# Attention in three units of 128-token chunks in place of four of 96, beside a PE-bound pair of feed-forward layers

## The chip, the core and the metric

The kernel runs on one core of one Trainium2 chip. The metric is the device time of one execution in microseconds. TensorE is called PE here, VectorE DVE, ScalarE ACT; SyncE (SP) issues the transfers.

## What is computed

Attention with pooled keys and values (each 8 tokens are averaged, so 576 tokens leave 72 keys), for 8 batches of 8 heads with a head size of 64, and then two feed-forward layers over all 4608 tokens, one with a leaky ReLU, one with a hard swish. All inputs are fp32, and the feed-forward products are made as three products of rounded parts (high x high, high x low, low x high).

```python
k_p = k.reshape(B, H, Sp, pool, D).mean(axis=3)
v_p = v.reshape(B, H, Sp, pool, D).mean(axis=3)
scores = scale * np.matmul(q, k_p.transpose(0, 1, 3, 2))
scores = scores - np.max(scores, axis=-1, keepdims=True)
attn = np.exp(scores)
attn = attn / (np.sum(attn, axis=-1, keepdims=True) + 1e-09)
attn_out = np.matmul(attn, v_p)
x = np.ascontiguousarray(attn_out.transpose(0, 2, 1, 3)).reshape(B * S, H * D)
h = x @ w_in;   x = np.maximum(0.01 * h, h) @ w_out
h = x @ w2_in;  y = (h * np.clip(h + 3.0, 0.0, 6.0) / 6.0) @ w2_out
```

## The kernel before

**Units.** `Unit(b, g, h)` is the attention of batch b, four heads (group g) and half of the tokens (h, 288 of 576). There are four to a batch, 32 in all. A unit has three chunks of `CQ` = 96 tokens. `scores` makes 12 small fp32 matmuls (3 chunks, 2 pairs of heads, 2 heads of a pair in the two halves of PE's rows), 96 queries as weights against 72 pooled keys, into two PSUM banks with the tag `a`. DVE takes the maxima (L484) and multiplies them by -1/64 (L489), ACT makes 12 exponentials with the sum of each row (L495, two instructions each: `ACTIVATE` and a read of the accumulator) into an SBUF tile `sm`, and DVE inverts the sums and scales the exponentials. `transposes` turns 64 of the 72 key columns (2 x 3 transposes, L545), `transpose_rem` the other 8 (3, L563), and `values` multiplies with the values (2 x 4 matmuls 288 wide, L590; in the first batch 2 x 2, one of them in full fp32).

**Preparation.** The first unit of a batch in each group (`fresh`) brings keys and values and pools them: `prep_k` reduces the keys into the group's one tile `keys`, and `prep_v` the values into `vbd` and `vrm`. The first batch pools its values on PE (`pool_v`, L400).

**Feed-forward layers.** A token tile of 512 tokens goes through 16 weight blocks f: `gemm1` (12 matmuls, L712 to L714) and `gemm2` (12, L761 to L763). The first two tiles start before their attention is whole: some blocks (`half0`, `half1` of them) are run first on the columns 0 to `HALF` and later on the rest, `HALF` to 512. The later tiles run in pairs with seven products in place of eight (`left_right`, L1016).

**Order.** The program is written as a list of tasks; `Plan.order` places them on the engines with assumed costs, so the order of each engine follows from the costs and from the slots in `C` at which attention steps are put between weight blocks (`att0` to `att7`, with the gaps of a unit's five steps). PE works strictly in its order. Up to the first `gemm2` the plan fills PE's expected idle time with matmuls on a tile of zeros (`plan.fill`, L1565), one for each 56 ns.

Of the kernel before, what the change touches and what calls it, by code (L numbers as in the profile page):

```python
# [21 lines left out]
POOL, SP = 8, 72  # L22
NF = DFF // 128
HALF, CQ, NC = 288, 96, 3
# [6 lines left out]
    n32=4,  # L31
    soon={0: 8000, 1: 4000},
    flex=562,
# [3 lines left out]
    when0=[0, 1, 0, 4, 9, 12, 17],  # L37
    att0=[0, 0, 13, 37],
    sec0=4,
    half1=4,  # L40
    steps1='frrffrfffffffrff',
    when1=[3, 15, 16, 20],
    att1=[0, 0, 27, 30],
    sec1=6,
    att2=[2, 4],
    quick=[0, 2, 2, 2, 2],
    slow=[0, 3, 3, 5, 3],
    left1=[[(0, 0), (1, 8)], [(2, 0), (3, 6)]],
    att3=[0, 0, 6, 9, 12, 13, 18, 21],
    gaps3=[0, 3, 3, 3, 0],  # L50
    prep3=[28, 37],
    att5=[5, 15, 24, 33, 42, 51, 60, 69],
    gaps5=[0, 7, 5, 11, 5],
    prep5=[77, 100],
    att7=[9, 24, 37, 55],
    gaps7=[2, 10, 10, 10, 12],
    prep7=[80, 85],
    left2=[[(0, 10)], [(1, 17)], [(2, 32)], [(3, 26), (4, 44), (5, 60)], [(6, 5), (7, 37)]],
)
SCORES = 1200  # L60
# [190 lines left out]
def attention_moe_moe(ctx: ExitStack, tc: tile.TileContext, qt, kt, vm, vr, wt, wq, eye, mask, out):  # L251
# [82 lines left out]
    class Unit:  # L334


        def __init__(self, b, g, h):
            self.b, self.g, self.h = b, g, h
            self.fresh = h == 0
            self.early = b == 0 and h == 0  # L340
            self.tag = "sb" if (g and b < 5) else "s"
            self.whole32 = None

# [17 lines left out]
    def fetch(u):  # L361
        if u.early:
            for i in range(2):
                load(half_k(u, i), kt[u.b, u.g, :, 576 * i : 576 * i + 576], 294912)
        elif u.fresh:
            load(u.k, kt[u.b, u.g], 589824)
        load(u.q, qt[u.b, u.g, u.h], 294912)
        if u.fresh:
            load(u.v, vm[u.b, u.g], 524288)
            load(u.r, vr[u.b, u.g], 196608)  # L370
# [21 lines left out]
    def pool_v(u):  # L392

        ps = buf("h", [128, 512], F32, 2, psum)
        u.vs, u.rs = ps("v", lambda t: t[:, 0:128]), ps("r", lambda t: t[:CQ, 128:192])
        for src, dst, n in ((u.v, u.vs, 128), (u.r, u.rs, 64)):

            def emit(src=src, dst=dst, n=n):
                for i in range(POOL):
                    PE.matmul(  # L400
                        out=dst.ap(),
                        lhsT=ident.ap()[: dst.ap().shape[0], : dst.ap().shape[0]],
                        rhs=src.ap()[:, i * n : i * n + n],
                        start=i == 0,
                        stop=i == POOL - 1,
                    )

            on_pe(1740 if n == 128 else 1320, emit, [src, ident], [dst])

    held_keys, held_values = {}, {}  # L410

    def prep_k(u):
        held_keys[u.g] = u.b
        k = View(keys[u.g].buf, None, lambda t: t.rearrange("p a n -> p (a n)"))
        if u.early:
            for i in range(2):
                sum_pool(part(keys[u.g], i, lambda t, i=i: t[:, i, :]), half_k(u, i), 72)
        else:
            sum_pool(k, u.k, 144)

    def prep_v(u):
# [7 lines left out]
        for e in range(2):  # L429
            p = slice(64 * e, 64 * e + 64)  # L430
            s = View(u.vs.buf, u.vs.key, lambda t, p=p: pair(u.vs.cut(t))[p])
            if u.whole32:
                copy(part(u.whole32[0], e, lambda t, p=p: t[p, :, p]), s, 128, u.early)
                continue
# [19 lines left out]
    def scores(u):  # L454


        assert held_keys[u.g] == u.b
# [3 lines left out]
        sm = buf("sm", [CQ, 12], F32, 2)  # L461
        at = lambda: s.get()[:CQ, 0 : NC * 4 * SP].rearrange("p (c h k) -> p c h k", c=NC, h=4)
        pss = [buf("a", [128, 512], F32, 2, psum) for _ in range(2)]

        def emit():
            for c in range(NC):
                for pi in range(2):
                    for e, ps in enumerate(pss):
                        rows = slice(64 * e, 64 * e + 64)
                        PE.matmul(  # L470
                            out=ps.get()[:CQ, (2 * c + pi) * SP : (2 * c + pi) * SP + SP],
                            lhsT=u.q.ap()[rows, pi * HALF + c * CQ : pi * HALF + c * CQ + CQ],
                            rhs=keys[u.g].ap()[rows, pi, :],
# [4 lines left out]
        on_pe(SCORES, emit, [u.q, keys[u.g]], [ps() for ps in pss])  # L478
        for e, ps in enumerate(pss):
            s4 = lambda ps=ps: ps.get()[:CQ, 0:432].rearrange("p (c a k) -> p c a k", c=NC, a=2)  # L480
            m = mx(e, lambda t, e=e: t[:, :, e : e + 3 : 2])
            on_dve(
                432,
                lambda m=m, s4=s4: DVE.tensor_reduce(out=m.ap(), in_=s4(), op=ALU.max, axis=AX.X),  # L484
                [ps()],
                [m],
            )

            on_dve(6, lambda m=m: DVE.tensor_scalar_mul(m.ap(), m.ap(), -1.0 / 64.0), [m], [m])  # L489

            def exps(e=e, s4=s4):
                for c in range(NC):
                    for pi in range(2):
# [5 lines left out]
                            scale=1.0 / 64.0,  # L499
# [4 lines left out]
            add("act", 1782, exps, [ps(), m], [s(e), sm(e)])  # L504
        whole = [s(pi) for pi in range(2)]
        inv = buf("inv", [CQ, 12], F32, 2)()
        on_dve(12, lambda: DVE.tensor_scalar_add(inv.ap(), sm.get(), 1e-9), [sm()], [inv])
# [16 lines left out]
        flat = lambda: s.get()[:CQ, 0 : NC * 256]  # L524
# [10 lines left out]

    def transposes(u):
        u.t = []
        pss = []
        for pi in range(2):
# [3 lines left out]
            def emit(ps=ps, pi=pi):  # L543
                for c in range(NC):
                    PE.transpose(out=ps.get()[:, c * CQ : c * CQ + CQ], in_=u.p(c, pi), identity=ident.ap()[:CQ, :CQ])  # L545

            on_pe(281, emit, [*u.whole, ident], [ps()])
        for pi, ps in enumerate(pss):
            src = ps(None, lambda t: t[:, 0:HALF])
            if u.whole32:  # L550
                copy(u.whole32[1][pi], src, HALF, True)
# [6 lines left out]
    def transpose_rem(u):  # L558
        ps = buf("a", [128, 512], F32, 2, psum)

        def emit():
            for c in range(NC):
                PE.transpose(  # L563
                    out=ps.get()[:96, c * CQ : c * CQ + CQ],
                    in_=f32(u.rem.get()[:, c].rearrange("p a b -> p (a b)")),
                    identity=ident.ap()[:CQ, :CQ],
                )

        on_pe(277, emit, [u.rem(), ident], [ps()])
# [3 lines left out]
    def values(u, x, spill):  # L573
        assert held_values[u.g] == u.b
        vh, vl = [t() for t in vbd[u.g]]
        pss = []
        for pi in range(2):
            ps = buf("a", [128, 512], F32, 2, psum)
            pss.append(ps)
            if u.whole32:  # L580
                ops = [(u.whole32[0], u.whole32[1][pi])]
            else:
                th, tl = u.t[pi]
                ops = [(vh, th), (vh, tl), (vl, th)]
            ops = [(l, lambda l=l, pi=pi: l.ap()[:, pi, :], r) for l, r in ops]
            ops.append((vrm[u.g](), lambda pi=pi: vrm[u.g].get()[:, 128 * pi : 128 * pi + 128], u.tr))

            def emit(ps=ps, ops=ops):
                for i, (_, l, r) in enumerate(ops):
                    PE.matmul(out=ps.get()[:, 0:HALF], lhsT=l(), rhs=r.ap(), start=i == 0, stop=i == len(ops) - 1)  # L590

            on_pe(536 if len(ops) > 2 else 609, emit, [v for l, _, r in ops for v in (l, r)], [ps()])
        for pi, ps in enumerate(pss):
            k = 2 * u.g + pi

            if u.h == 0:
                dst = x((k, 0), lambda t, k=k: t[:, k, 0:HALF])
                copy(dst, ps(None, lambda t: t[:, 0:HALF]), HALF, True, 0.125)
            else:
                n = TOK - HALF  # L600
                dst = x((k, 1), lambda t, k=k: t[:, k, HALF:TOK])
                copy(dst, ps(None, lambda t, n=n: t[:, 0:n]), n, True, 0.125)
                dst = spill(k, lambda t, k=k: t[:, k, :])
                copy(dst, ps(None, lambda t, n=n: t[:, n:HALF]), REST, True, 0.125)
# [727 lines left out]
    def attend(jobs, u, slot, held, nxt, gaps):  # L1332
# [4 lines left out]
        def first():  # L1337
            scores(u)
# [4 lines left out]
        at(s[0], first)  # L1343
        at(s[1], lambda: transposes(u))
        at(s[2], lambda: transpose_rem(u))
        at(s[3], lambda: values(u, held["x"], held["spill"]))
        if nxt is not None:
            at(s[4], lambda: prepare(nxt))
# [6 lines left out]
    units = [Unit(b, g, h) for b in range(B) for h in range(2) for g in range(2)]  # L1355
# [4 lines left out]
    u0, u1, u2, u3 = units[:4]  # L1360
    place(u0)
    u1.q = a15("q", lambda t: t[:, 1296:1872])
    raw_k(u1, a15)
    raw_v(u1, a14)
    for u in units[: C["n32"]]:
        g = u.g
        a = a13 if g else a12
        v = a("v", lambda t: pair(t[:, 0:256]))
        u.whole32 = v, [a(("p", i), lambda t, i=i: t[:, 256 + 288 * i : 544 + 288 * i]) for i in range(2)]
        if u.early:  # L1370
            add("gp", 400, lambda v=v: GP.memset(v.ap(), 0.0), [], [v])
    u2.q, u3.q = a7("q2", lambda t: t[:, 0:576]), a7("q3", lambda t: t[:, 576:1152])
# [41 lines left out]
    fetch(u3)  # L1414
# [21 lines left out]
    attend_all(jobs, (2, 3), C["att0"][:2], held, QUICK)  # L1436
# [17 lines left out]
    attend_all(jobs, (4, 5), C["att0"][2:], held, SLOW)  # L1454
# [9 lines left out]
    attend_all(jobs, (6, 7), C["att1"][:2], held, QUICK)  # L1464
# [3 lines left out]
    attend_all(jobs, (8, 9), C["att1"][2:], held, SLOW)  # L1468
# [9 lines left out]
    attend_all(jobs, (10, 11), C["att2"], held, SLOW)  # L1478
# [11 lines left out]
    def attend_batch(jobs, b, slots, gaps, store, begin=None, chain=False):  # L1490

        held = {}
        units_of = units[4 * b : 4 * b + 4]
# [18 lines left out]
        for n, (u, slot) in enumerate(zip(units_of, slots), 1):  # L1512
            nxt = units_of[n] if n < 4 else units[4 * b + 4] if chain else None
# [23 lines left out]
    attend_batch(jobs, 3, C["att3"][:4], C["gaps3"], True, chain=True)  # L1537
    held = attend_batch(jobs, 4, C["att3"][4:], C["gaps3"], False)
# [7 lines left out]
    attend_batch(jobs, 5, C["att5"][:4], C["gaps5"], True, 0, True)  # L1546
    held = attend_batch(jobs, 6, C["att5"][4:], C["gaps5"], False)
# [76 lines left out]
```

## Time and profile before

| | |
|---|---|
| runs | 1585.05, 1589.53, 1590.87 us |
| median | 1589.53 us |
| span of the profiled execution | 1583.1 us |
| its own time | the page doesn't give it; the runs lie 2.0 to 7.8 us above the span |
| PE busy | 1572.4 us (99%), 8312 matmul passes |
| DVE busy | 1184.9 us (75%) |
| ACT busy | 999.7 us (63%) |
| granted clock of PE | 1.000 of 2.4 GHz over the span |

A matmul's recorded length holds its way through the array, so lengths of neighbours overlap and "busy" can hide small waits. What an instruction costs PE in a row of its like is the distance between two starts. Attention is spread over the first 653 us; the rest of the span is feed-forward work alone.

### The profile page before, as it was taken

The numbers are of one execution on the slowest core, as the hardware profiler recorded it, in microseconds if no ns is written. First come the engines' busy times: TensorE is split into PE (matmuls) and PEld (weight loads), VectorE is DVE, ScalarE is ACT, GpSimd is POOL, SyncE is SP. The second block draws the span as 40 slices with busy tenths as digits, with TensorE's granted clock in tenths as the row PEclk, the third lists the DMA queues.
The fourth block names the chain that finished last, engine by engine and source line by source line (L and its number), as shares of the span: only waits on it lengthen the run. The fifth ranks groups of instructions, "written<-read, shape, count | busy, mean of one in ns | idle before, by whom it ended". The sixth has DMA issues, their size and how long they took to land.

```text
span 1583.1 us, 23979 instructions
## 1 busy us (share of the span) xinstructions
PE 1572.4 (99%) x8312; PEld 1347.5 (85%) x8312; DVE 1184.9 (75%) x2139; ACT 999.7 (63%) x2480; POOL 2.3 (0%) x12
## 2 busy tenths in 40 slices
PE   9999999999999999999999999999999999999999
PEld 8888888887888788888888888888898888889988
DVE  7998778678989876995687569568846865885494
ACT  7878677677977578766655455446545554654454
POOL 0000000000000000000000000000000000000000
PEclk9999999999999999999999999999999999999999
DMA  8888677667897799979977567756865775676564
GB/s 293 313 317 298 232 263 272 225 225 268 282 310 236 264 333 321 317 270 323 322 272 251 184 229 244 256 206 219 283 227 206 251 264 205 221 252 227 207 239 146
DMA packets 129481, 406.40 MB, mean 257 GB/s; under 512 B 18640, under 2 KB 47440, under 8 KB 107600
## 3 DMA queue, kind: packets, MB, share of 16 engines
q1 hardware_dynamic: 129360, 404.87, 74.2%
q8 instruction: 66, 1.08, 0.3%
q14 instruction: 55, 0.45, 0.1%
HBM read 317.79 MB, written 87.03 MB: 256 GB/s over the span
## 4 chain that ended last, share of the span: by engine, by line
PE 90%; DVE 5%; ACT 3%; DMA 2%; issue 1%; SPq 0%; ACTq 0%; DVEq 0%
PE y L1016 35%; PE h L1016 22%; PE a L1016 12%; PE y L761 3%; PE y L763 3%; PE y L762 3%; PE h L712 3%; PE h L714 2%; PE h L713 2%; PE a L470 2%; PE a L590 2%; DVE w L883 1%; ACT s L495 1%; PE a L545 1%; DMA raw<-vr 1%; PE idle L1565 1%
## 5 line engine op out<-in xcount | busy, mean ns | idle before, releaser
L883 DVE TENSOR_TENSOR w<-y,w 128x512 f32<-128x512 f32 (+2 forms) x108 | 71.1, 658 | 107.7 <-PE y L1016 104.2
L309 ACT ACTIVATE gh<-w 128x460 fp32r<-128x460 f32 (+1 forms) x140 | 82.3, 589 | 65.2 <-PE y L1016 31.6
L883 DVE TENSOR_TENSOR w<-w 128x460 f32<-128x460 f32 (+2 forms) x168 | 105.2, 648 | 3.1 <-ACT w L727 2.8
L1211 DVE SCALAR_TENSOR_TENSOR gl<-w,gh 128x460 fp32r<-128x460 f32 (+1 forms) x140 | 88.8, 635 | 23.5 <-ACT gh L309 22.9
L1016 PE MATMUL y<-w,xh 128*128 128x512 f32 (+2 forms) x444 | 104.2, 384 | 0.0
L495 ACT ACTIVATE s<-a,mx 96x72 f32<-96x72 f32 x264 | 79.6, 323 | 27.7 <-DVE mx L489 27.7
L1016 PEld LDWEIGHTS y<-w,xh 128*128 128x128 f32 x444 | 82.6, 188 | 13.5
L1182 ACT ACTIVATE gh<-w,three 128x460 f32<-128x460 f32 (+1 forms) x60 | 40.9, 682 | 70.6 <-DVE w L883 70.6
L761 PE MATMUL y<-gh,w 128*128 128x512 f32 (+2 forms) x220 | 85.2, 387 | 0.0
L1016 PE MATMUL y<-w,raw 128*128 128x460 f32 (+1 forms) x384 | 83.2, 370 | 0.0
L306 ACT CAST gh<-w 128x512 fp32r<-128x512 f32 x96 | 59.5, 622 | 35.8 <-PE y L1016 23.4
L712 PE MATMUL h<-xh,w 128*128 128x512 f32 (+2 forms) x220 | 81.5, 371 | 0.0
L763 PE MATMUL y<-gh,w 128*128 128x512 f32 (+2 forms) x220 | 80.6, 366 | 0.0
L714 PE MATMUL h<-xh,w 128*128 128x512 f32 (+2 forms) x220 | 80.5, 366 | 0.0
L713 PE MATMUL h<-xl,w 128*128 128x512 f32 (+2 forms) x220 | 80.4, 365 | 0.0
L762 PE MATMUL y<-gl,w 128*128 128x512 f32 (+2 forms) x220 | 80.3, 365 | 0.0
L1016 PEld LDWEIGHTS y<-w,raw 128*128 128x128 f32 x384 | 72.1, 188 | 7.9
L1016 PE MATMUL y<-w,xl 128*128 128x512 f32 (+2 forms) x324 | 76.7, 385 | 0.0
L316 DVE TENSOR_TENSOR gl<-w,gh 128x512 fp32r<-128x512 f32 x96 | 65.6, 685 | 14.5 <-ACT gh L306 14.4
L316 DVE TENSOR_TENSOR st<-raw,st 128x512 fp32r<-128x512 f32 x88 | 59.7, 684 | 13.8 <-ACT st L306 13.2
L1016 PE MATMUL y<-gh,raw 128*128 128x462 f32 (+1 forms) x224 | 69.4, 371 | 0.0
L1016 PEld LDWEIGHTS y<-w,xl 128*128 128x128 f32 x324 | 60.5, 188 | 10.5
(257 smaller groups left out, 4250.9 us busy)
## 6 DMA issues: line engine op xcount, KB each, us to landing
raw<-left SPq DMA_DIRECT2D x68, 1024.0 KB, 4.8
left<-st SPq DMA_DIRECT2D x176, 256.0 KB, 4.3
xh<-left SPq DMA_DIRECT2D x37, 1024.0 KB, 4.8
xl<-left SPq DMA_DIRECT2D x68, 512.0 KB, 4.9
xh<-left SPq DMA_DIRECT2D x56, 512.0 KB, 5.1
w<-left SPq DMA_DIRECT2D x56, 512.0 KB, 5.2
xl<-left SPq DMA_DIRECT2D x25, 1024.0 KB, 4.8
w<-wt SPq DMA_DIRECT2D x16, 1024.0 KB, 7.6
```

The source lines that it names most:

```text
L309: a = lambda: ACT.mul(out=dst.ap(), in_=src.ap(), mul=scale)
L316: lambda: DVE.tensor_tensor(out=dst.ap(), in0=a.ap(), in1=f32(b.ap()), op=ALU.subtract),
L495: ACT.activation(out=at()[:, c, h, :], in_=s4()[:, c, pi, :], func=AF.Exp, scale=1.0 / 64.0, bias=mx.get()[:, c, h : h + 1], accum_out=sm. ...
L712: PE.matmul(out=o, lhsT=hi, rhs=xh.get()[:, k, c0:c1], start=k == 0, stop=False)
L713: PE.matmul(out=o, lhsT=hi, rhs=xl.get()[:, k, c0:c1], start=False, stop=False)
L714: PE.matmul(out=o, lhsT=lo, rhs=xh.get()[:, k, c0:c1], start=False, stop=k == 3)
L761: PE.matmul(out=y[:, n0:n1], lhsT=hi, rhs=gh.get()[:, n0:n1], start=start, stop=False)
L762: PE.matmul(out=y[:, c0:c1], lhsT=hi, rhs=gl.get()[:, c0:c1], start=False, stop=False)
L763: PE.matmul(out=y[:, c0:c1], lhsT=lo, rhs=gh.get()[:, c0:c1], start=False, stop=stop)
L883: on_dve(n, lambda: DVE.tensor_tensor(out=dst.ap(), in0=a.ap(), in1=b.ap(), op=op), [a, b], [dst])
L1016: PE.matmul(out=o, lhsT=l, rhs=r, start=first and i == m == 0, stop=last and i == len(left) - 1 and m == 2, skip_group_check=True,)
L1211: lambda: DVE.scalar_tensor_tensor(out=lo.ap(), in0=v.ap(), scalar=1.0 / 6.0, in1=f32(hi.ap()), op0=ALU.mult, op1=ALU.subtract),
```

## The change

**Units.** `Unit(b, n)` now has three to a batch, 24 in all, of 384 tokens x 4 heads each: n = 0 and 1 are the first 384 tokens of the groups 0 and 1, and n = 2 (the tail unit) is the last 192 tokens (`TAIL`) of both groups. A chunk has 128 tokens. The tail unit has two chunks of group 0 or 1 and one of 64 tokens of each, so its scores are 8 matmuls with 128 weight columns and 8 with 64, and its values are 16 matmuls 192 wide, in two groups of columns of one bank.

**Scores.** The factor 1/64 moves from the exponential's scale into the pooled keys (a copy with a factor in `prep_k`, which reduces into `ks` first). The maxima come out negated, and the multiplication at L489 is gone. The sums of the exponentials go to 12 columns of the first score bank in place of an SBUF tile. The second unit's scores use the banks `y2` and `y3`.

**The rest.** `HALF` goes from 288 to 384, and with it the split of the first two token tiles; `half1` goes from 4 to 3, `n32` from 4 to 3. The planner's costs and all slots in `C` are new. The queries are laid out on the host for the new units.

```diff
-HALF, CQ, NC = 288, 96, 3
+HALF, CQ, NC = 384, 128, 3
+TAIL = S - HALF
...
-    half1=4,
+    half1=3,
...
+            sum_pool(mid_, src, n)
+            dst = View(keys[u.g].buf, None if i is None else i, lambda t, i=i: t.rearrange("p a n -> p (a n)") if i is None else t[:, i, :])
+            copy(dst, mid_, n, scale=1.0 / 64.0)
...
+        if u.n == 2:
+            blocks = [(slice(0, 128), c, c, 128 * c) for c in range(2)]
+            blocks += [(slice(64 * g, 64 * g + 64), 2, g, 256 + 64 * g) for g in range(2)]
+        else:
+            blocks = [(slice(0, 128), c, u.g, 128 * c) for c in range(NC)]
...
-                lambda m=m, s4=s4: DVE.tensor_reduce(out=m.ap(), in_=s4(), op=ALU.max, axis=AX.X),
-                [ps()],
+                lambda m=m, s4=s4: DVE.tensor_reduce(out=m.ap(), in_=s4(), op=ALU.max, axis=AX.X, negate=True),
+                [ps("s")],
...
-            on_dve(6, lambda m=m: DVE.tensor_scalar_mul(m.ap(), m.ap(), -1.0 / 64.0), [m], [m])
...
-                            accum_out=sm.get()[:, 4 * c + h : 4 * c + h + 1],
+                            accum_out=pss[0].get()[:, 440 + 4 * c + h : 440 + 4 * c + h + 1],
...
+            def emit(ps=ps, groups=groups):
+                for c0, n, ops in groups:
+                    for i, (_, l, r) in enumerate(ops):
+                        PE.matmul(
+                            out=ps.get()[:, c0 : c0 + n], lhsT=l(), rhs=r.ap()[:, c0 : c0 + n], start=i == 0, stop=i == len(ops) - 1
+                        )
...
+    u1.banks = [("y2", 1), ("y3", 1)]
...
-    att0=[0, 0, 13, 37],
+    att0=[0, 14, 44],
...
-    att5=[5, 15, 24, 33, 42, 51, 60, 69],
+    att5=[9, 19, 32, 43, 54, 62],
```

**Where instructions stand now.** First place: ACT in the opening. The names: `s` and `sb` hold the exponentials of the first and the second unit, `a` and `y` are PSUM banks, the 1024-wide rows decode the first weight block. Before:

```order
L495 ACTIVATE s_186,sm_187<-a_164,mx_180 96x72 x6
L495 ACTIVATE s_186,sm_187<-a_166,mx_180 96x72 x6
L626 ACTIVATE w_1_70<-w_1_96 128x1024
L306 CAST rem_324<-rn_321 96x3x32 x2
L628 ACTIVATE w_1_74<-w_1_96 128x1024
L495 ACTIVATE sb_347,sm_348<-a_306,mx_341 96x72 x6
L495 ACTIVATE sb_347,sm_348<-a_308,mx_341 96x72 x6
```

Now:

```order
L312 ACTIVATE keys_1_191<-w_1_95 128x72
L512 ACTIVATE s_196,a_172<-a_172,mx_189 128x72 x6
L512 ACTIVATE s_196,a_172<-a_174,mx_189 128x72 x6
L512 ACTIVATE sb_283,y_1_247<-y_1_247,mx_278 128x72 x6
L309 CAST rem_302<-rn_299 128x3x32 x2
L512 ACTIVATE sb_283,y_1_247<-y_1_249,mx_278 128x72 x6
L659 ACTIVATE w_1_70<-w_1_267 128x1024
L309 CAST vrm_1_362<-raw_203 96x256
L661 ACTIVATE w_1_74<-w_1_267 128x1024
```

Both units' exponentials stand ahead of the weight block now, with only a rounding between them; before, the decoding stood between the two units. The first row is a scaling of the second unit's keys.

Second place: PE where one batch gives way to the next, in the stage with pairs (about 440 us into the span before). `keys` are the pooled keys, `th`, `tl` and `tr` the transposed exponentials, `vbd` and `vrm` the values; `h` and `y` rows are feed-forward work, six matmuls each. Before:

```order
L470 MATMUL a_5428<-keys_1_91,q_5297 96x72
L1016 MATMUL h_5442<-w_2_4391,w_6_4639 128x512 x6
L1016 MATMUL h_5456<-w_2_4391,w_6_4639 128x512 x6
L1016 MATMUL y_8_5390<-w_2_4663,w_6_4639 128x512 x6
L590 MATMUL a_5490<-th_5362,vbd_1_84 128x288
L590 MATMUL a_5490<-tl_5372,vbd_1_84 128x288
L590 MATMUL a_5490<-th_5362,vbd_1_86 128x288
```

Now:

```order
L619 MATMUL a_4875<-th_4818,vbd_1_84 128x192
L619 MATMUL a_4875<-tl_4831,vbd_1_84 128x192
L619 MATMUL a_4875<-th_4818,vbd_1_86 128x192
L619 MATMUL a_4875<-tr_4849,vrm_1_394 128x192
L1049 MATMUL h_4666<-w_2_4121,xl_4074 128x512 x6
L1049 MATMUL y_8_4902<-w_2_4029,xl_4074 128x512 x6
L487 MATMUL a_4918<-keys_1_92,q_4755 128x72
```

Before, the next batch's first scores (the first row there is their last matmul) stood ahead of the last unit's values; now they stand behind the tail unit's values, with twelve feed-forward matmuls between. The filler matmuls, of which the whole order has 248 before, are 208 now.

## Rows read from the trace of the kernel before

**Rows 1.** The page: span, busy time of the engines, chain that ended last.

```profile
span 1583.1 us, 23979 instructions
PE 1572.4 (99%) x8312; PEld 1347.5 (85%) x8312; DVE 1184.9 (75%) x2139; ACT 999.7 (63%) x2480; POOL 2.3 (0%) x12
...
PE 90%; DVE 5%; ACT 3%; DMA 2%; issue 1%; SPq 0%; ACTq 0%; DVEq 0%
```

**Rows 2.** Stretches: length, busy us by engine (instructions), clock, DMA share, GB/s.

```profile
0.00:51.00 51.00, 46.22 (x528) 41.88 (x529) 39.80 (x84) 39.09 (x146) 1.98 (x11) 1.00 0.80 281
51.00:350.00 299.00, 298.60 (x1816) 250.58 (x1815) 241.68 (x471) 218.39 (x725) 0.28 (x1) 1.00 0.77 269
350.00:650.00 300.00, 298.30 (x1632) 241.60 (x1631) 248.52 (x469) 232.64 (x715) 0.00 (x0) 1.00 0.86 289
650.00:1583.00 933.00, 929.29 (x4341) 813.45 (x4340) 654.88 (x1118) 509.59 (x897) 0.00 (x0) 1.00 0.70 241
```

**Rows 3.** PE in order of time, opening: start us, us, instruction, [idle <-releaser].

```profile
0.98 5.66 PE L1565 MATMUL idle<-zeros 128*128 128x128 bf16 x66 [0.98 <-DVE three L1381]
...
7.75 5.53 PE L1565 MATMUL idle<-zeros 128*128 128x128 bf16 x96
...
17.75 1.50 PE L400 MATMUL h<-w,ident 96*96 96x64 f32 x16
19.08 0.42 PE L545 MATMUL a<-ident,s 96*128 96x96 f32 x3
19.33 1.98 PE L400 MATMUL h<-w,ident 128*128 128x128 f32 x16
21.15 0.41 PE L563 MATMUL a<-ident,rem 96*96 96x96 f32 x3
...
24.19 0.72 PE L590 MATMUL a<-w 128*128 128x288 f32 x2 [1.06 <-ACT tr L306]
```

**Rows 4.** PE in order of time around one unit's scores.

```profile
299.00 0.40 PE L763 MATMUL y<-gh,w 128*128 128x512 f32 x1
299.32 1.24 PE L470 MATMUL a<-keys,q 64*96 64x72 f32 x24
300.50 0.50 PE L712 MATMUL h<-xh,w 128*128 128x512 f32 x1
300.83 0.40 PE L713 MATMUL h<-xl,w 128*128 128x512 f32 x1
```

**Rows 5.** PE in order of time around six transposes.

```profile
169.14 0.66 PE L545 MATMUL a<-ident,s 96*128 96x96 f32 x6
169.58 0.48 PE L712 MATMUL h<-xh,w 128*128 128x512 f32 x1
169.90 0.40 PE L713 MATMUL h<-xl,w 128*128 128x512 f32 x1
...
172.24 0.39 PE L714 MATMUL h<-xh,w 128*128 128x512 f32 x1
```

**Rows 6.** PE in order of time: values, then 224-wide matmuls.

```profile
189.96 0.30 PE L590 MATMUL a<-th,vbd 128*128 128x288 f32 x1
...
190.49 0.41 PE L545 MATMUL a<-ident,sb 96*128 96x96 f32 x3
...
190.99 0.27 PE L763 MATMUL y<-gh,w 128*128 128x224 f32 x1
...
192.11 0.41 PE L545 MATMUL a<-ident,sb 96*128 96x96 f32 x3
```

**Rows 7.** ScalarE in order of time, the first exponentials.

```profile
9.14 0.32 ACT L495 ACTIVATE s<-a,mx 96x72 f32<-96x72 f32 x1 [6.92 <-DVE mx L489]
...
9.45 0.30 ACT L495 ACTIVATE s<-a,mx 96x72 f32<-96x72 f32 x1
```

**Rows 8.** VectorE, groups by line and shape: count, busy us, mean ns, idle before.

```profile
L376 DVE TENSOR_REDUCE keys<-raw 128x144 f32<-128x1152 f32 x14 | 18.8, 1344 | 1.8 <-DMA raw<-kt 1.6
```

More of the change, by code (lines that the diff above doesn't have):

```diff
@@ L334, in attention_moe_moe, with __init__, columns @@
     class Unit:
[L337 to L341, printed above, removed]
+        def __init__(self, b, n):
+            self.b, self.n = b, n
+            self.groups = (0, 1) if n == 2 else (n,)
+            self.fresh = n < 2
+            self.g = n if n < 2 else None
+            self.early = b == 0 and n < 2
+            self.tag = "sb" if (3 * b + n) % 2 and b < 5 else "s"
+            self.banks = None
             self.whole32 = None
+        def columns(self):
+            return [(g, TAIL * i, TAIL) for i, g in enumerate(self.groups)] if self.n == 2 else [(self.g, 0, HALF)]
     def raw_k(u, a):
@@ L454, in scores @@
     def scores(u):
-        assert held_keys[u.g] == u.b
+        assert all(held_keys[g] == u.b for g in u.groups)
         s = buf(u.tag, [128, 1024])
@@ L476, in emit @@
                         )
-        on_pe(SCORES, emit, [u.q, keys[u.g]], [ps() for ps in pss])
+        on_pe(SCORES, emit, [u.q, *(keys[g] for g in u.groups)], [ps("s") for ps in pss])
+        sums = [pss[0](("m", e), lambda t, e=e: t[:, 440 + e : 452 + e]) for e in range(2)]
         for e, ps in enumerate(pss):
-            s4 = lambda ps=ps: ps.get()[:CQ, 0:432].rearrange("p (c a k) -> p c a k", c=NC, a=2)
+            s4 = lambda ps=ps: ps.get()[:, 0:432].rearrange("p (c a k) -> p c a k", c=NC, a=2)
             m = mx(e, lambda t, e=e: t[:, :, e : e + 3 : 2])
@@ L550, in transposes @@
             if u.whole32:
-                copy(u.whole32[1][pi], src, HALF, True)
+                copy(u.whole32[pi], src, HALF, True)
                 continue
@@ L573, in values @@
     def values(u, x, spill):
-        assert held_values[u.g] == u.b
-        vh, vl = [t() for t in vbd[u.g]]
+        assert all(held_values[g] == u.b for g in u.groups)
         pss = []
+        columns = u.columns()
         for pi in range(2):
@@ L579, in values @@
             pss.append(ps)
[L580 to L592, printed above, removed]
+            groups = []
+            for g, c0, n in columns:
+                if u.whole32:
+                    ops = [(whole_v[g], u.whole32[pi])]
+                else:
+                    th, tl = u.t[pi]
+                    vh, vl = [t() for t in vbd[g]]
+                    ops = [(vh, th), (vh, tl), (vl, th)]
+                ops = [(l, lambda l=l, pi=pi: l.ap()[:, pi, :], r) for l, r in ops]
+                ops.append((vrm[g](), lambda g=g, pi=pi: vrm[g].get()[:, 128 * pi : 128 * pi + 128], u.tr))
+                groups.append((c0, n, ops))
+            def emit(ps=ps, groups=groups):
[4 more added lines that the diff above has]
+                        )
+            cost = sum((4 * n / 2.4 + pe_cost(n) + 8 if u.whole32 else 4 * pe_cost(n) + 8) for _, n, _ in groups)
+            on_pe(cost, emit, [v for _, _, ops in groups for l, _, r in ops for v in (l, r)], [ps()])
         for pi, ps in enumerate(pss):
-            k = 2 * u.g + pi
-            if u.h == 0:
+            if u.n < 2:
+                k = 2 * u.g + pi
                 dst = x((k, 0), lambda t, k=k: t[:, k, 0:HALF])
```

168 lines of the change are left out of this document (90 added, 78 removed).

## The prediction

> **What bounds the kernel now.** I read the page's busy times first. TensorE (PE) is busy for 1572.4 of the 1583.1 us of the span, VectorE for 75% and ScalarE for 63%, and PE makes up 90% of the chain that ended last [rows 1]. So PE's own work sets the time, and whatever VectorE or ScalarE save is worth only what PE waits for them. The second view cuts the span into stages [rows 2]: PE lacks 4.78 us of being busy in the first 51 us, 0.40 us from there to 350, 1.70 us to 650, and 3.71 us in the last stage, which has almost no attention. The clock is 1.00 in all four. The third view is the opening in order of time [rows 3]. PE starts with 66 and then 96 filler matmuls (L1565, on a tile of zeros), work that the plan puts where it expects PE to wait. Before the first attention values PE still waits 1.06 us for ScalarE. So the opening is bound by ScalarE, VectorE and transfers, and everything behind it by PE. An edit has to be costed as PE work, except in the opening.
>
> Three prices follow from these views. The reader takes the distance from one start to the next, since the recorded lengths overlap. A 512-wide matmul of the feed-forward part costs 0.234 us (ten of them, 169.90 to 172.24) [rows 5]. A 288-wide one costs 0.1325 (0.53 us for four), and a 224-wide one 0.112 (1.12 us for ten) [rows 6]. The line through 512 and 288 has a slope of 0.00045 us a column, so it gives 0.176 for 384 columns, 0.104 for 224, 0.089 for 192 and 0.060 for 128. The 224-wide row already lies above that line, as if something other than the columns set it.
>
> **The change, part by part.** The span is 1583.1 us; the page doesn't give that execution's own time. The runs lie 2.0 to 7.8 us above it and their median, 1589.53, 6.4 us. I take those 6.4 us as unchanged, so a sum in the span is a sum in the median.
>
> *Scores.* A unit's 12 fp32 matmuls are 24 passes, in twelve pairs that use both halves of the rows. They take 1.18 us from 299.32 to 300.50. The row ahead of them is 0.32 us before them instead of 0.23, and the first row behind holds for 0.33 us instead of 0.23, so the insertion costs 1.18 + 0.09 + 0.10 = 1.37 us [rows 4]. For the price of a pass as its weights grow, the nearest rows are the two kinds of pooling matmul: 16 passes with 96 weight columns take 1.33 us (0.083 each), 16 with 128 columns 1.82 us (0.114) [rows 3]. Twelve pairs have eleven steps, 11 x 0.083 = 0.91, which leaves 0.46 for the edges; that fits a price set by the weight columns. So a full unit will take 11 x 0.114 + 0.46 = 1.71 us. The tail unit has eight pairs of 128 columns and eight of 64: 7 x 0.114 + 8 x (0.06 to 0.083) + 0.46, plus up to 0.2 for a second change of the block's shape, the size of the two edges above. That is 1.74 to 2.12; I take 1.93. A batch costs 2 x 1.71 + 1.93 = 5.35 in place of 4 x 1.37 = 5.48, and eight batches **-1.0 us**. If the weight columns cost nothing it would be -8 us, at the dear end +0.5.
>
> The Trainium skill ("TensorE: Matmul & The Clock Gate", Part 2, LDWEIGHTS) says that a weight load's time goes by its columns alone, and gives columns / 1.2 ns: 80 ns for 96 and 107 ns for 128, near the 83 and 114 of the pooling rows. By it the batch loads 48 x 96 = 4608 columns before and 32 x 128 + 8 x 64 = 4608 after, so larger chunks would save nothing but edges. The skill ("TensorEngine Tiling", Key Properties) also says that a change of tiling mode drains the engine, which speaks against the tail unit's two block sizes; the 0.09 and 0.10 us of the edges agree with it.
>
> *Transposes.* Six take 0.44 us, and the row behind them lasts 0.086 us too long (0.32 instead of 0.234): 0.526 / 6 = 0.088 us each [rows 5]. There were 32 x 9 = 288, there will be 24 x 9 = 216, each with 128 identity columns in place of 96. If the price goes by the count it is -72 x 0.088 = -6.3 us; if it goes by the columns, 0. No row has 128 of them, so I take the middle, **-3.2 us**.
>
> *Values.* The columns stay the same (32 x 288 = 16 x 384 + 16 x 192 a batch), but 192-wide matmuls are narrower than 224, and I price them like the 224-wide row: 7 batches x (16 x 0.176 + 16 x 0.112 - 32 x 0.1325) = **+2.6 us**. On the line (0.089) it would be 0. The first batch uses a two-pass form whose columns are unchanged; I take 0 for it.
>
> *The split of the first two tiles.* Here the chunk's size reaches the feed-forward part, since HALF is also the first part of the token tile. Seven weight blocks (half0 = 3, half1 = 4) were run as 288 + 224 columns, 24 matmuls each; six will be run as 384 + 128, and the seventh whole. Before: 7 x 24 x (0.1325 + 0.112) = 41.1 us. After: 24 x (6 x (0.176 + 0.112) + 0.234) = 47.1, with the 128-wide ones at the price of the 224-wide. The matmuls that open the tiles' sums are 512 wide both times, which takes 8 x (0.176 - 0.1325) = 0.35 off. **+5.7 us**; if a 128-wide one costs 0.060, -1.8.
>
> *The opening.* The order has 208 fillers in place of 248. 96 of them take 5.53 us, 0.058 each [rows 3], so 40 are worth -2.3 us. Beside that PE had 4.78 us of idle [rows 2]. ScalarE's first exponentials waited 6.92 us for the maxima [rows 7], and each exponential with its read of the sum takes 0.31 us, so twelve take 3.6. The second unit's scores now go to banks of their own, the extra multiplication of the maxima is gone, and the weight decoding moved behind both units' exponentials. I take -0.7 us for the idle, **-3.0 us** together. The ends are -7 (fillers and all idle) and +2 (the first weights, which now land and are decoded later, come late).
>
> *The rest.* A quarter fewer units means fewer exponentials and multiplications, and the waits of 51 to 650 us are 2.1 us by the busy times [rows 2]: **-1.0 us**, between -2 and +3. The sums in PSUM, whatever they cost ScalarE, and the extra scaling of the keys lie beside PE work here: nothing. The queries are the same bytes in 24 transfers in place of 32.
>
> Sum: -1.0 - 3.2 + 2.6 + 5.7 - 3.0 - 1.0 = +0.1. The span stays at 1583.2 and the median at **1589.6 us**. The attention saves what the split gives back.
>
> **The rivals.** *B, faster: narrow matmuls have no floor.* If 128 and 192 columns follow the line, the split falls from +5.7 to -1.8 and the values from +2.6 to 0: 10.1 us less, 1579.5 us. For it: a filler, 128 columns wide with 128 weight columns, takes 0.058 us. Against it: that is bf16, and the 224-wide row lies 0.008 above the line at the 0.112 that 128 four-byte weight columns cost in the pooling rows. The Trainium skill ("TensorE: Matmul & The Clock Gate", Back-to-back issue gap) gives columns / 2.4 + 2.5 ns, which is 56 ns for 128 columns: the filler agrees, the 224-wide row (96 by that rule) doesn't. Chance 0.13.
>
> *C, slower: PE waits where batches meet.* The tail unit reads the keys and values of both head groups. So the next batch's keys can't be put in place before its scores, nor values before its values, and the next scores stand in PE's order behind the tail unit's values, where they stood ahead of the last unit's values before. PE works in order, so such a wait stops the feed-forward matmuls queued behind the scores. Twelve 512-wide matmuls (2.8 us) lie between at the narrowest places. It decides if VectorE is later than that; where the reduction of the keys (1.344 us [rows 8]) and a copy of some 0.3 us stand unfinished, the price is 1.6 us x 7 boundaries = 11.2, 1600.8 us. Against it: the reduction itself can run earlier, and VectorE has 25% to spare. Chance 0.08.
>
> *D, the change doesn't reach the time.* Everything that it takes off ScalarE and VectorE was hidden, and PE's columns are the same: that is the forecast itself, short of the split. If the split cost nothing and the transposes saved nothing, it would be 1587; this lies in the forecast.
>
> **How the numbers follow.** About 0.5% (8 us) is what a measurement can tell from no change. Forecast with D: 0.72. Faster: B 0.13, and 0.05 for transposes, scores and opening all near their cheap ends: 0.18. Slower: C 0.08, and 0.02 for late first weights: 0.10. The range reaches from B's 1579 to just below C's time, 1598.
>
> **What would show it.** 128-wide and 192-wide rows about 0.112 us apart (B: 0.06 and 0.09); pairs of score passes 0.114 apart; transposes between 0.08 and 0.11; PE idle under 5 us up to 51 us and under 2 us from there to 650; no wait of PE for keys. It would be wrong if the narrow rows come faster, or if PE's idle time in 51 to 650 us grows by more than 5 us.

## The result, and the profile after

The changed kernel takes 1603.4 us (median of four runs, 1600.35 to 1604.49) against 1588.2 us before (1585.05 to 1590.87). The ratio is 1.0092, with a 95% interval of 1.0074 to 1.011. I had forecast 1589.6 us and no change, with a range from 1579 to 1598, so the forecast was wrong. The span grew from 1583.1 to 1601.0 us.

The page after: span, busy time of the engines, chain that ended last.

```profile
span 1601.0 us, 23002 instructions
PE 1575.8 (98%) x8048; PEld 1348.6 (84%) x8048; DVE 1159.1 (72%) x2001; ACT 991.0 (62%) x2235; POOL 2.1 (0%) x12
...
PE 72%; DVE 12%; ACT 7%; DMA 6%; issue 2%; SPq 0%; ACTq 0%; DVEq 0%
```

Beside [rows 1] the chain has changed most. PE is busy for as long as before, within 3.4 us, but its share of the chain fell from 90% to 72%; VectorE rose from 5% to 12% and ScalarE from 3% to 7%. Both of these engines have less to do than before and still set the end more often. The stages say where (the columns are those of [rows 2]: length, busy us of PE, of its weight loads, of VectorE, ScalarE and POOL with instructions, clock, DMA share, GB/s):

```profile
0.00:51.00 51.00, 47.22 (x474) 43.38 (x475) 38.29 (x71) 38.98 (x122) 1.91 (x11) 1.00 0.77 275
51.00:350.00 299.00, 292.64 (x1643) 243.83 (x1641) 222.31 (x393) 209.32 (x597) 0.20 (x1) 1.00 0.75 260
350.00:650.00 300.00, 289.27 (x1530) 234.93 (x1531) 229.31 (x403) 224.02 (x607) 0.00 (x0) 1.00 0.83 282
650.00:1601.00 951.00, 946.69 (x4405) 826.44 (x4403) 669.17 (x1138) 518.67 (x910) 0.00 (x0) 1.00 0.70 242
```

The clock is 1.00 in all four. In the two stages that hold the attention PE is idle for 6.36 and 10.73 us, where it was 0.40 and 1.70. That is 15 of the 18 us. The opening, which was to gain, lost only 1.0 us of its idle time (3.78 for 4.78).

What PE waits for, in the list of its waits (us in total, times, longest us):

```profile
PE a L587 <- DVE tl L319: 3.2, 4, 0.9
PE a L569 <- DVE sb L543: 3.2, 3, 1.6
PE a L569 <- DVE s L543: 2.9, 4, 0.9
...
PE a L619 <- ACT s L512: 2.1, 1, 2.1
```

The first three are transposes (L569, L587) that wait for the scaled exponentials or for what is made of them. The last is a unit's values (L619), which write a PSUM bank that the next unit's exponentials still read. No wait for keys is in the list. ScalarE in order of time, the first three exponentials, answers [rows 7]:

```profile
10.07 0.32 ACT L512 ACTIVATE s<-a,mx 128x72 f32<-128x72 f32 x1 [1.36 <-DVE mx L503]
10.29 0.16 ACT L512 ACTIVATION_READ_ACCUMULATOR s<-a,mx 128x1 f32 x1
10.48 0.32 ACT L512 ACTIVATE s<-a,mx 128x72 f32<-128x72 f32 x1
10.70 0.16 ACT L512 ACTIVATION_READ_ACCUMULATOR s<-a,mx 128x1 f32 x1
10.89 0.32 ACT L512 ACTIVATE s<-a,mx 128x72 f32<-128x72 f32 x1
```

An exponential now starts 0.41 us after the one ahead of it; in [rows 7] the step was 0.31, and over all exponentials of before its median is 0.296 us, of after 0.415. Yet the read of the sum has become shorter, 0.16 us for 0.19. The first read of before, which stands between the two lines of [rows 7]:

```profile
9.36 0.19 ACT L495 ACTIVATION_READ_ACCUMULATOR s<-a,mx 96x1 f32 x1
```

The time lies between the start of the read and the start of the next ACTIVATE: 0.19 us (10.29 to 10.48), where it was 0.09 (9.36 to 9.45). The order of the instructions, with the semaphores that each waits for, names the reason. Before:

```
L495 ACTIVATE s_186,sm_187<-a_164,mx_180 96x72 [waits DVE_49,PE_49]
L495 ACTIVATE s_186,sm_187<-a_164,mx_180 96x72 x5
```

After:

```
L512 ACTIVATE s_196,a_172<-a_172,mx_189 128x72 [waits DVE_49]
L512 ACTIVATE s_196,a_172<-a_172,mx_189 128x72 [waits Activation_49] x5
```

`Activation_49` is ScalarE's own semaphore. Each exponential writes its sum into the score bank `a_172`, so the next one, which writes the same bank and in the first six of a unit reads it too, is made to wait until that write is reported. With 288 exponentials it is 288 x (0.415 - 0.296) = 34 us more of ScalarE's time. The plan, on the other hand, has six exponentials at 1.56 us (`EXPS`), 0.26 each. The old plan had 1.782, which is 0.297 each and what the chip takes. So a unit's twelve exponentials end 12 x (0.415 - 0.26) = 1.9 us later than the order was made for.

What that does can be seen near 60 us. First ScalarE after, in order of time, the first and the last of one unit's twelve exponentials and what follows them:

```profile
59.12 0.34 ACT L512 ACTIVATE sb<-a,mx 128x72 f32<-128x72 f32 x1
...
63.70 0.32 ACT L512 ACTIVATE sb<-a,mx 128x72 f32<-128x72 f32 x1
63.97 1.13 ACT L659 ACTIVATE w<-w 128x1024 f32<-128x1024 f32 x1
```

VectorE in order of time behind them:

```profile
64.11 0.17 DVE L523 TENSOR_SCALAR inv<-a 128x12 f32<-128x12 f32 x1 [1.61 <-ACT sb L512]
...
65.12 1.23 DVE L664 SCALAR_TENSOR_TENSOR w<-w,w 128x1024 int32<-128x1024 int32 x1 [0.52 <-ACT w L659]
...
66.64 0.95 DVE L543 TENSOR_TENSOR sb<-sb,inv 128x768 f32<-128x768 f32 x1
```

And PE, which needs the last of these:

```profile
65.72 0.39 PE L796 MATMUL y<-gh,w 128*128 128x512 f32 x1
67.73 0.85 PE L569 MATMUL a<-ident,sb 128*128 128x128 f32 x6 [1.63 <-DVE sb L543]
```

The twelve exponentials take from 59.12 to 63.97. VectorE has waited 1.61 us for the last of them. Behind them on ScalarE stands the decoding of a weight block (L659), now as late as they are; VectorE's step of that decoding (L664) stands ahead of the scaling of the exponentials (L543) and has to wait for it. So the scaling ends at 67.6, and PE, which works in its order, stands still for 1.63 us.

### The profile page after: what moved, and what is told of

It is laid out like the page before. It is cut to its first block, busy times and chain, and to the rows that moved or that the text cites. A ratio compares the mean times of both kernels' runs of the same rounds, so it can differ in the third digit from the quotient of the medians.

```text
span 1601.0 us, 23002 instructions
## 1 busy us (share of the span) xinstructions
PE 1575.8 (98%) x8048; PEld 1348.6 (84%) x8048; DVE 1159.1 (72%) x2001; ACT 991.0 (62%) x2235; POOL 2.1 (0%) x12
## 4 chain that ended last, share of the span: by engine, by line
PE 72%; DVE 12%; ACT 7%; DMA 6%; issue 2%; SPq 0%; ACTq 0%; DVEq 0%
PE y L1049 29%; PE h L1049 17%; PE a L1049 12%; ACT s L512 4%; DMA left<-st 3%; DVE w L916 2%; PE y L794 2%; PE y L796 2%; PE y L795 2%; PE a L619 2%; PE h L747 1%; PE h L746 1%; PE h L745 1%; DVE gl L319 1%; ACT sb L512 1%
## 5 line engine op out<-in xcount | busy, mean ns | idle before, releaser
L309 ACT CAST st<-raw 128x512 fp32r<-128x512 f32 x88 | 54.4, 621 | 36.3 <-DMA left<-st 17.3
L512 ACT ACTIVATE s<-a,mx 128x72 f32<-128x72 f32 x204 | 65.4, 321 | 16.4 <-DVE mx L503 10.3
```

Source lines behind the costliest of these rows:

```text
L309: a = lambda: ACT.copy(out=dst.ap(), in_=src.ap())
L512: ACT.activation(out=at()[:, c, h, :], in_=s4()[:, c, pi, :], func=AF.Exp, bias=mx.get()[:, c, h : h + 1], accum_out=pss[0].get()[:, 440 + ...
```

## The experiments

In all of them the kernel before ran beside (1588 to 1589 us). E1 to e3 and e6 to e8 are edits of the changed kernel, e4 and e5 of the kernel before.

### The sums back in SBUF, nothing else changed

```diff
+        sm = buf("sm", [CQ, 12], F32, 2)
...
-                            accum_out=pss[0].get()[:, 440 + 4 * c + h : 440 + 4 * c + h + 1],
+                            accum_out=sm.get()[:, 4 * c + h : 4 * c + h + 1],
...
-        on_dve(12, lambda: DVE.tensor_scalar_add(inv.ap(), pss[0].get()[:, 440:452], 1e-9), sums, [inv])
+        on_dve(12, lambda: DVE.tensor_scalar_add(inv.ap(), sm.get(), 1e-9), [*sums, sm()], [inv])
```

> The changed kernel with the sums of the exponentials in an SBUF tile again; the order of every engine and all else as in the changed kernel. Theory 1 (each exponential waits for ScalarE's own read of the sum when that goes to PSUM, 0.41 us apart in place of 0.30, so a unit's exponentials end 1.4 us later and PE waits for them): exponentials about 0.30 us apart, PE's idle time in 51 to 650 us back from 17 to under 6 us, time 1584 to 1590 us. Rival (tail units and batch boundaries make PE wait, whatever the exponentials cost): PE's idle time stays over 12 us, time 1598 us or more.

Measured: 1580.9 us, ratio to before 0.9953 (0.9935 to 0.9972). Every engine has the same instructions in the same order as in the changed kernel, so 22.5 us hang on where the sums go. The stages of this kernel up to 650 us:

```profile
0.00:51.00 51.00, 49.60 (x490) 46.07 (x491) 41.66 (x75) 39.59 (x127) 1.91 (x11) 1.00 0.83 289
51.00:350.00 299.00, 297.54 (x1700) 249.89 (x1699) 226.25 (x400) 204.00 (x614) 0.20 (x1) 1.00 0.78 265
350.00:650.00 300.00, 299.00 (x1548) 243.65 (x1547) 241.32 (x421) 223.51 (x612) 0.00 (x0) 1.00 0.88 295
```

PE's idle time is 1.40, 1.46 and 1.00 us. The median step of the exponentials is 0.296 us again, and the transposes that stood still for 1.63 us follow at once on the row ahead of them (PE in order of time):

```profile
62.39 0.40 PE L797 MATMUL y<-gh,w 128*128 128x512 f32 x1
62.71 0.85 PE L570 MATMUL a<-ident,sb 128*128 128x128 f32 x6
```

This version beats both kernels: 0.5% below before, and below the 1584 to 1590 us that I expected of it.

### Sums in SBUF, true price, placed anew

```diff
-EXPS = 1560
+EXPS = 1782
```

(and the sums no longer held in the score bank, for the plan too)

> As e1, but the plan also knows it: six exponentials are priced 1.782 us as in the kernel before, in place of 1.56, and the score bank is free again after the exponentials, so the order is planned anew with the same slots. Theory 1: within 4 us of e1 (1582 to 1590), a little faster if what waits are left come from the price of 1.56, which is 0.2 us below what six take. Rival (unit structure): 1598 or more.

Measured: 1584.7 us, 0.9977 (0.9965 to 0.9988). PE's idle time is 1.75, 0.47 and 6.70 us in the three stages: another plan for the same slots places a few waits of its own. Differences of about 4 us between two plans are therefore not to be read as more than that.

### Sums in PSUM, but with their true price in the plan

```diff
-EXPS = 1560
+EXPS = 2490
```

> The changed kernel with the sums in PSUM as they are, but the plan knows what they cost: six exponentials priced 2.49 us (0.415 each) in place of 1.56, order planned anew with the same slots. If the loss is only that PE's order was made for exponentials that end 1.9 us earlier than they do, this order hides them behind feed-forward work: 1585 to 1592. If ScalarE's extra time itself (0.12 x 288 = 34 us) is what costs, it stays at 1598 or more.

Measured: 1586.5 us, 0.9985 (0.9974 to 0.9996). ScalarE does here what it does in the changed kernel, with the step of 0.415 us, and 17 of the 22.5 us are back. Two of its stages:

```profile
51.00:350.00 299.00, 297.46 (x1663) 250.19 (x1664) 227.15 (x399) 211.05 (x603) 0.21 (x1) 1.00 0.75 258
350.00:650.00 300.00, 298.40 (x1574) 243.81 (x1573) 236.72 (x414) 229.18 (x622) 0.00 (x0) 1.00 0.87 295
```

PE is idle for 1.54 and 1.60 us. So for the most part it isn't ScalarE's extra 34 us that costs, but that the order did not reckon with them. The score bank, too, is held here until VectorE has read the sums, as in the changed kernel, so that hold is not what costs the 17 us. Of the 5.6 us that are not back, 5.2 are fillers in the opening: the plan puts 283 of them, which take 20.2 us with what is idle behind them, where e1 has 208 with 15.0. There the longer exponentials may still cost; no run tests that by itself.

### The kernel before with its sums in PSUM

```diff
-                            accum_out=sm.get()[:, 4 * c + h : 4 * c + h + 1],
+                            accum_out=pss[0].get()[:CQ, 440 + 4 * c + h : 440 + 4 * c + h + 1],
```

> The kernel before with one part of the change alone: the sums go to 12 columns of the first score bank; the order of every engine is that of the kernel before. Theory 1: exponentials 0.41 us apart here too, 1.4 us later in each of 32 units against a plan that prices them right for SBUF: PE waits 0.3 to 0.8 us a unit, 1598 to 1612 us. Rival (unit structure): 1588, no change.

Measured: 1639.0 us, 1.0315 (1.0295 to 1.0335). The direction was right, the size wrong: 51 us instead of 10 to 24. The step of the exponentials is 0.408 us. From the first lines of PE's waits:

```profile
PE a L545 <- ACT sb L495: 14.2, 6, 3.4
PE a L590 <- ACT s L495: 8.1, 5, 2.6
...
PE a L470 <- ACT s L495: 3.0, 3, 1.3
PE a L590 <- ACT sb L495: 2.8, 1, 2.8
```

Transposes, values and scores wait here for the exponentials themselves, 28.1 us in all. PE's idle time up to 650 us is 40.0 us, where it was 6.9. The granted clock is lower, too: 0.97 to 0.98 up to 650 us, where it is 1.00 before. Next to waits of PE of 1.9 to 3.4 us it falls to 0.50 (1.2 GHz), for 27 us in all, and 512-wide matmuls are then 0.427 us apart instead of 0.231. PE stands still for 9 of these 27 us, so I estimate the clock's part from these rows at 18 x (1 - 0.231 / 0.427) = 8 us. The 10 us that are left of the 51 I can't place.

### The kernel before with sums in PSUM and their true price

```diff
-            add("act", 1782, exps, [ps(), m], [s(e), sm(e)])
+            add("act", 2490, exps, [ps("s"), m], [s(e), sums[e]])
```

(the sums in the first score bank, as in the fourth experiment, and the plan told so)

> The kernel before (chunks of 96) with its sums in PSUM, as in e4_before_sums_psum, but with the sums named to the plan as users of the score bank and six exponentials priced at 2.49 us in place of 1.78, so that the work is placed anew. If it is the mismatch of the plan with the chip that cost 51 us there, 1585 to 1600 us, with PE idle under 5 us in 51 to 650 us (30.0 in e4). If it is ScalarE's longer time itself, which no order can hide, 1615 to 1640.

Measured: 1616.4 us, 1.017 (1.0145 to 1.0194). 23 of the 51 us are back, 28 are not, so in this kernel the price alone doesn't do it. PE's idle time in the two stages, 13.02 and 3.75 us, is 13 us less than in e4 and far from before:

```profile
51.00:350.00 299.00, 285.98 (x1700) 237.70 (x1701) 232.99 (x457) 218.50 (x688) 0.28 (x1) 0.98 0.73 249
350.00:650.00 300.00, 296.25 (x1630) 240.39 (x1630) 240.09 (x456) 232.85 (x697) 0.00 (x0) 1.00 0.82 274
```

The expectation for the mismatch (1585 to 1600) was missed, and the rival's lower end was met. With 32 units a kernel has 384 exponentials, 384 x (0.408 - 0.296) = 43 us more on ScalarE in place of 34. I read the 13.02 us as these slots leaving no room for them between 51 and 350 us, but that is not shown: whether other slots would was not tried.

### The sum's place, measured by itself

Eight rows of twelve exponentials, nothing else on ScalarE, in one run; the sums of five of the rows go to

```python
...
    run(es[1], lambda i: sm[:, i : i + 1])
    run(es[2], lambda i: sq[:, 0:1])
    run(es[3], lambda i: other[:, 440 + i : 441 + i])
    run(es[4], lambda i: one[:, 440 + i : 441 + i])
    run(es[5], lambda i: pairs[i % 2][:, 440 + i : 441 + i])
...
```

where `sm` and `sq` are in SBUF, and `other` (the bank that is read), `one` and `pairs` are PSUM banks.

> Leaves the whole computation out: ScalarE alone runs eight rows of twelve exponentials 128x72 out of one PSUM bank, each row with its sums put elsewhere: none; SBUF, a column for each; SBUF, all into one column; the bank that is read; one other bank; two banks in turn; three banks in turn; and SBUF with 96 partitions. My theory says that it is the wait on the preceding read of the sum that costs, and not the write into PSUM: then a step is 0.29 to 0.31 us with SBUF columns, 0.40 to 0.42 with the bank that is read and with one other bank, and also with one SBUF column (within 0.05 of the PSUM rows); with two banks in turn about 0.30, since the wait there is for the read before the last, and with three the same. The rival says that it is PSUM itself (its write is slow to be seen): then one SBUF column takes 0.30 as its neighbours do, and two and three banks in turn take 0.41. A second rival, that 128 partitions take longer than 96: the last row would be shorter than the second by over 0.03.

ScalarE in order of time: one step each of SBUF columns, one SBUF column, the bank that is read, and two banks in turn.

```profile
7.06 0.41 ACT L42 ACTIVATE e<-other,bias 128x72 f32<-128x72 f32 x1
7.36 0.42 ACT L42 ACTIVATE e<-other,bias 128x72 f32<-128x72 f32 x1
...
10.93 0.32 ACT L42 ACTIVATE e<-other,bias 128x72 f32<-128x72 f32 x1
11.37 0.32 ACT L42 ACTIVATE e<-other,bias 128x72 f32<-128x72 f32 x1
...
16.23 0.32 ACT L42 ACTIVATE e<-other,bias 128x72 f32<-128x72 f32 x1
16.65 0.32 ACT L42 ACTIVATE e<-other,bias 128x72 f32<-128x72 f32 x1
...
25.64 0.32 ACT L42 ACTIVATE e<-other,bias 128x72 f32<-128x72 f32 x1
25.89 0.34 ACT L42 ACTIVATE e<-other,bias 128x72 f32<-128x72 f32 x1
```

The steps are 0.295 us with SBUF columns, 0.44 with one SBUF column, 0.415 with the bank that is read and with one other bank, 0.254 with two banks and with three, and 0.295 with 96 partitions. Without a sum it is 0.204. So it is the wait on the sum just ahead that costs, 0.15 us in SBUF and 0.16 in PSUM, and not PSUM, which is 0.04 us faster than SBUF without that wait and 0.03 with it. For two banks I had expected 0.30, so that PSUM is the faster place was a surprise. (The last four steps of the two banks' row are 0.273.) The plan's 0.26 fits that 0.254, a PSUM sum without a wait on the one just ahead, which the kernel as written never gets. The Trainium skill ("ScalarE: Activation LUTs", Step-by-step: what each stage is for) calls PSUM the faster destination for ScalarE; the trace agrees, by the 0.254 against 0.295 and the 0.415 against 0.44, and the 0.415 against 0.295 shows that a wait for the write outweighs it.

### Sums in SBUF with a price that is too low

```diff
-EXPS = 1560
+EXPS = 1080
```

(the sums in SBUF, as in the second experiment)

> The changed kernel with its sums in SBUF and six exponentials priced at 1.08 us, which is as far below what they take with SBUF sums (1.78) as the kernel's 1.56 was below what they took with PSUM sums (2.49, 0.9 below). If the mismatch of price and chip alone makes PE wait, 1592 to 1605 us, with PE idle over 10 us in 51 to 650 us. If the sums in PSUM must be there (the time that ScalarE spends, whatever the plan), 1581 to 1588, with PE idle under 8 us as in e2_after_sums_sbuf_replanned.

Measured: 1604.7 us, 1.0091 (1.0065 to 1.0116). No sum is in PSUM here and an exponential takes 0.296 us, yet the time is that of the changed kernel. The stages:

```profile
51.00:350.00 299.00, 290.09 (x1643) 242.10 (x1641) 225.29 (x398) 203.68 (x607) 0.20 (x1) 1.00 0.76 259
350.00:650.00 300.00, 293.01 (x1542) 237.22 (x1541) 227.47 (x397) 215.42 (x604) 0.00 (x0) 1.00 0.83 279
```

PE is idle for 8.91 and 6.99 us (after: 6.36 and 10.73). An order made for exponentials that end too early is enough by itself. (The price is 0.7 us below what six take, and not 0.9, as the expectation reckons.)

### Sums in two score banks in turn

```diff
-                            accum_out=pss[0].get()[:, 440 + 4 * c + h : 440 + 4 * c + h + 1],
+                            accum_out=pss[pi].get()[:, 440 + 2 * c + e : 440 + 2 * c + e + 1],
```

> The changed kernel, its sums still in PSUM and every instruction of TensorE in the same order, but the sums of successive exponentials go in turn to the two score banks of the unit, and two additions of six columns read them in place of one of twelve. If the wait of each exponential on the read just before it is the whole cause, a step takes 0.25 to 0.26 us as with two banks in turn in m1_where_the_sum_goes (0.254), six take about 1.53 us, which is what the plan has as their price (1.56), and the time is 1577 to 1584, at or a little below e1_after_sums_sbuf (1580.9), with PE idle under 5 us in the first 650 us. If sums in PSUM cost the kernel something else (the bank held until the sums are read, the extra reading by VectorE), 1588 to 1604.

> As e7_after_two_banks, but both banks are named to the plan as holding sums until these are read, so that the work is placed a little anew (some 330 lines of TensorE's order stand elsewhere). The price of an exponential in the plan is the true one, so my theory gives 1578 to 1588, with a few us for how the new placing falls; the other reading 1588 to 1604.

Two additions of six columns read the sums here, and the second version also names both banks to the plan. Measured: 1605.2 us, 1.0102 (1.0085 to 1.0119), and placed anew 1607.6 us, 1.0114 (1.0092 to 1.0135). My expectation was wrong, for a plain reason that ScalarE's rows show (the same instructions as in the second view of after):

```profile
10.11 0.32 ACT L512 ACTIVATE s<-a,mx 128x72 f32<-128x72 f32 x1
...
10.52 0.32 ACT L512 ACTIVATE s<-a,mx 128x72 f32<-128x72 f32 x1
```

The median step is still 0.415 us. In the measurement by itself none of the two or three banks that took sums in turn was read by an exponential; here the two score banks are the ones that are read, and every exponential that follows another is still given the wait on the one ahead. So neither run tests what two banks are worth in this kernel. They do show that the time stays where it was as long as the step and the price stay.

### Together

The lateness is six times the measured step less the plan's price for six, in us:

| kernel | step | price of six | lateness | time, us |
|---|---|---|---|---|
| before | 0.296 | 1.78 | 0.0 | 1588.2 |
| e2: SBUF, true price | 0.296 | 1.78 | 0.0 | 1584.7 |
| e3: PSUM, true price | 0.415 | 2.49 | 0.0 | 1586.5 |
| e1: SBUF | 0.296 | 1.56 | 0.2 | 1580.9 |
| e6: SBUF, price too low | 0.296 | 1.08 | 0.7 | 1604.7 |
| after | 0.415 | 1.56 | 0.9 | 1603.4 |
| e7, e8: two banks | 0.415 | 1.56 | 0.9 | 1605.2, 1607.6 |
| e4: before, PSUM | 0.408 | 1.78 | 0.7 | 1639.0 |
| e5: before, PSUM, true price | 0.408 | 2.49 | 0.0 | 1616.4 |

In the seven versions of the changed kernel the time goes by the lateness, with a few us for the plan, and not by the step or the place of the sums. E1 lies lowest although its price is 0.2 too low: that much the order bears. In the kernel before, lateness explains a part alone: e5 has none and is still 28 us slower than before.

## Why the prediction was wrong, point by point

**The step that failed** is in "The rest": "The sums in PSUM, whatever they cost ScalarE, and the extra scaling of the keys lie beside PE work here: nothing." I gave no price for a sum in PSUM and no bounds, and the only cover that I could point to was the time that ScalarE had to spare (37% by [rows 1]). That share is an average. PE's order holds the transposes at one place, and the cover there is the distance that the plan left, which is worked out from the plan's price. The term measured +22.5 us (after against e1). The new wait stands in the changed order; I had read that order without its waits. The step in [rows 7] was 0.31 us and `EXPS` gave 0.26; I did not ask how the price could be lower than the row.

**The other terms** can be read from e1, which has everything but the sums in PSUM. I summed the distance from each PE instruction's start to the next one's, over all records of a function, in us:

| term | before | e1 | difference | predicted | after |
|---|---|---|---|---|---|
| scores | 38.1 | 36.3 | -1.8 | -1.0 | 35.9 |
| transposes | 22.2 | 20.1 | -2.1 | -3.2 | 20.7 |
| values | 36.7 | 37.7 | +1.0 | +2.6 | 38.4 |
| first tiles (split) | 277.4 | 281.6 | +4.2 | +5.7 | 290.9 |
| fillers and what is idle behind them | 18.1 | 15.0 | -3.1 | -3.0 | 15.7 |
| pooling of values | 6.4 | 6.4 | 0 | | 7.4 |
| pairs of tiles | 1179.3 | 1176.5 | -2.8 | -1.0 (the rest) | 1187.3 |

The sum is -4.6 us where I had +0.1, so without the sums in PSUM the kernel would have come out at 1581 and inside my range. The medians lie further apart, 7.3 us. Every run since lies 1.8 us above its own span, so the profiled execution of before took about 1585 us, some 3 less than the median, and my 6.4 us between span and median was for the most part that.

The row of the fillers holds only the idle time behind them. Of the opening's idle time before, 0.9 us stands under the transposes, 0.9 under the values and 0.2 under the first tiles. Put in its place, the opening gives -5.1 us (predicted -3.0), the transposes -1.2 (-3.2), the values +1.9 (+2.6) and the split +4.4 (+5.7). So none of the five priced terms is off by more than 2.1 us.

A wait counts with the row ahead of it, which is why the 22 us of after appear under the first tiles (+9.3 against e1) and the pairs (+10.8). What took 2.8 us off the pairs in e1 I can't name.

- *Scores, transposes, values, split.* PE after in order of time at four places: the split's 128-wide rows, values 192 wide, a unit's scores between feed-forward rows, values 384 wide:

```profile
48.36 0.28 PE L746 MATMUL h<-xl,w 128*128 128x128 f32 x1
48.47 0.28 PE L747 MATMUL h<-xh,w 128*128 128x128 f32 x1
...
312.77 0.27 PE L619 MATMUL a<-tl,vbd 128*128 128x192 f32 x1
312.88 0.27 PE L619 MATMUL a<-th,vbd 128*128 128x192 f32 x1
...
317.00 0.39 PE L747 MATMUL h<-xh,w 128*128 128x512 f32 x1
317.31 1.56 PE L487 MATMUL a<-keys,q 64*128 64x72 f32 x24
318.81 0.50 PE L794 MATMUL y<-gh,w 128*128 128x512 f32 x1
...
400.75 0.34 PE L619 MATMUL a<-th,vbd 128*128 128x384 f32 x1
400.92 0.34 PE L619 MATMUL a<-tl,vbd 128*128 128x384 f32 x1
```

  A 384-wide step is 0.17 to 0.18 us (predicted 0.176), a 192-wide one 0.11 and a 128-wide one 0.11 (both predicted 0.112): the floor of the narrow matmuls is there and rival B is false. (The pooling rows give 0.114 for 128 weight columns, not the 0.112 that I quoted there.) The scores of a full unit take 1.50 us from their start to the next row's, against 1.18 before [rows 4], and pairs are 0.112 apart as predicted (0.114). The 64-column pairs of the tail unit are cheaper than I had them: 2.1 us for the 56 steps between them in e1, 0.038 each, in place of 0.06 to 0.083. Transposes with 128 identity columns are 0.109 us apart, where those with 96 were 0.082 by the median of all (I had 0.088 from one place [rows 5]); so the price goes by the columns, the end of my bounds that gives nothing; of the 2.1 us that still fell, 0.9 is idle time of the opening, and the rest I put down to fewer edges, which no run separates.
- *The opening.* e1 takes 3.4 us off its idle time (1.40 for 4.78) where I had 0.7, and the fillers give 1.7 where I had 2.3: the way was right, the size of the idle time too small. In after most of it is undone: its opening is idle for 3.78.
- *Rival C.* It put the slowdown at 1600.8 us, close to the time, with a wait of PE for keys where batches meet. The list of PE's waits of after has none, so its time was close by chance and its mechanism false. No rival held the sums' wait, and all that was slower had a chance of 0.10 together.
- *What would show it wrong.* The last sign that I named, idle time in 51 to 650 us up by more than 5 us, is what came: 17.1 us for 2.1.

## What to carry to other kernels

When an edit moves an operand, list what each instruction waits for, before and after: a sum that goes into a bank which the next instruction reads turns a stream without waits into a chain. Where a plan with assumed prices fixes the order, an engine with a third of its time to spare has no cover beyond what the prices leave, so hold each price against the measured step (0.26 against 0.296 or 0.415 here) before anything is called hidden. And try a change that bundles several edits with each of them taken out: one line here hid a gain of 7 us behind a loss of 22.5.

## What was unexpected of the hardware

- An exponential 128x72 takes 0.204 us without a sum, 0.254 with its sum in PSUM and no wait on the sum just ahead, 0.295 with the sum in SBUF, 0.415 in PSUM with the wait on the sum ahead, and 0.44 in SBUF with it. ScalarE's wait on its own last write costs 0.15 to 0.16 us for each exponential here, more than the place of the write.
- 96 and 128 partitions take the same 0.295 us with the sum in SBUF, so a chunk of 128 tokens gives a third more exponentials in a step.
- The recorded length of the read of a sum (0.16 to 0.5 us) says little of its cost: in the row with three banks in turn it grows from 0.31 to 0.51 us while the step stays at 0.254.
